# A fused sparse attention and gated MLP on one Trainium2 core: first pair loaded whole, another mask chain, mask rows by GpSimd and in query halves, in-projection dealt through the batch change

## The chip, the cores and the metric

The kernel runs on one core of a Trainium2 chip. A core has TensorE (PE, the matmuls; its weight loads are shown as PEld), VectorE (DVE), ScalarE (ACT), GpSimd (POOL) and SyncE (SP, which here only issues DMAs). Each engine executes its own instructions in the order in which they were emitted and waits on semaphores for the others. The metric is the device time of one execution in microseconds. Lower is better.

## What is computed

Block-sparse attention over 4 batches x 8 heads of 768 positions with head dimension 64, then a gated MLP with a spatial product. `sampled_blocks` gives three more allowed key blocks for each of 24 query blocks.

```python
scores = scale * np.matmul(q, k.transpose(0, 1, 3, 2))
mask = np.abs(blk_i - blk_j) <= window            # blocks of 32, window 1
mask = mask | (blk_i == 0) | (blk_j == 0) | (blk_i == n_blocks - 1) | (blk_j == n_blocks - 1)
for qb in range(n_blocks):
    for kb in sampled_blocks[qb]:
        mask[qb * block:(qb + 1) * block, kb * block:(kb + 1) * block] = True
scores = np.where(mask, scores, -1000000000.0)
attn = softmax(scores)
x = (attn @ v), heads side by side                # 768 x 512 for each batch
h = np.maximum(x @ w_in, 0.0)                     # 768 x 1024
u, v = h[..., :512], h[..., 512:]
v_n = (v - mean(v)) / np.sqrt(var(v) + 1e-06)
v_s = np.einsum('ts,bsd->btd', w_spatial, v_n) + b_spatial[None, :, None]
out = (u * v_s) @ w_out
```

## The kernel before

**Layout.** `qt_all` and `kt_all` hold, for each of 8 heads, the transposed queries and keys: rows 0 to 63 are the head dimension, rows 64 to 87 carry the mask. The mask is computed inside the score matmul: the 24 rows of k are the indicator of the key's block (`ind`), the 24 rows of q are the product of `bm` (24x24, 0 where allowed and -300 where not) with the indicator (the matmuls into `mq`). One score matmul has therefore 88 rows. The rows are the same for all heads, so head 0 gets them from ACT and the other heads are copied from head 0: heads 1 to 3 of k and 1 to 5 of q by DVE (`mask_rows`, L574), the others by DMAs on SP's queue (`mask_dma`, L579).

**The start.** Head 0 and head 1 of k and q are loaded one by one: the two of head 0 on ACT's queue, the others on SP's, behind the sampled blocks. `cast_qk` makes bf16 of them (q's head 0 on DVE, k's on ACT, head 1 of both on POOL), `tr_head` transposes on PE into a PSUM bank and copies to `kt_all` or `qt_all` on DVE. `keep_warm` issues matmuls whose result is not used. The mask chain on DVE runs from `ind` through `edge`, `diff` and `allowed` (three steps, one for each sampled block) to `bm` (L238).

**The first batch** is worked through in two query halves of 384 columns: 48 steps `g` of `qk_exp_half` (two score matmuls into one PSUM tile of two, L348, and one exponential on ACT, L352), with `av_half` six steps later (L364), the normalisation by the softmax sum on DVE (`rc` L375, `xn` L376) and at given steps the transposes of the next pairs (`tr_slots`, copies on DVE at L278) and of the results (`xtr_half`, L385 and the copy L386). From step 29 each step also issues one unit of the first MLP.

**The other three batches** are worked through by pairs of heads, 12 steps a pair: `qk_exp` (L313, exponential L317), `av` seven steps later (L329), `norm` (L394, L395). Pairs are loaded, cast by POOL (`prepare`, L124 and L127), transposed by DMA on SP's queue (`tr_dma`) and split into `kt_all` and `qt_all` by DVE (`split_pair`, L302, at s = 7 and 9 of the pair before). Step 48 (`N0`) is the first of the second batch.

**The MLP** of a batch is a list of units, `moe_q`, each one matmul of 512 columns (L472): 12 in-projection products of 4 units (v for the second half of the columns, u for the first), 6 spatial products of 6, 6 out-projection products of 4. They take turns over two PSUM banks. A v product is evicted to `vsb` by DVE (L485), followed by `stats` (L488) and `mv` (L489); after three v products POOL makes `rstd` (L492, L494) and three normalisations (`vn`, L499) are put into `norm_q` with the product count from which they may be emitted; they are emitted one at a time, in the middle of a product or after a u product. A u product is evicted by ACT (L509), the first of batch 0 by DVE (L506). The order of the products is a string for each batch. How many units a step gets follows from `slots_left`, which spreads the units left evenly:

```python
            if g == N0 + 7:
                slots_left = 50
            if moe_q and slots_left > 0:
                budget += len(moe_q) / slots_left
                slots_left -= 1
                while moe_q and budget >= 0.5:
                    moe_q.popleft()()
```

So no unit is issued in steps 48 to 54. The last batch's MLP follows after the last step, over more PSUM banks.

Of the kernel before, what the change touches and what calls it, by code (L numbers as in the profile page):

```python
# [10 lines left out]
FP32 = mybir.dt.float32  # L11
BF16 = mybir.dt.bfloat16
I32 = mybir.dt.int32
# [13 lines left out]
def kernel(  # L27
# [146 lines left out]
    nc.scalar.dma_start(out=stk[:, 0:1], in_=dram(k, 0, 0, 1))  # L174
    nc.scalar.dma_start(out=stq[:, 0:1], in_=dram(q, 0, 0, 1))
    nc.sync.dma_start(out=samp_i, in_=_listify(sampled_blocks).bitcast(I32))
    nc.sync.dma_start(out=stk[:, 1:2], in_=dram(k, 0, 1, 1))
    nc.sync.dma_start(out=stq[:, 1:2], in_=dram(q, 0, 1, 1))
# [6 lines left out]
    allowed = const.tile([NB, NB], FP32)  # L185
    tiny = const.tile([128, 1], FP32)
    nc.vector.memset(warm, 0.0)
    nc.gpsimd.memset(ind_nat, 0.0)
# [5 lines left out]
    def keep_warm(n, cols):  # L194
        for _ in range(n):
# [3 lines left out]
    keep_warm(8, 512)  # L199
# [4 lines left out]
    nc.gpsimd.affine_select(out=ind_nat, in_=ind_nat, compare_op=ALU.not_equal, fill=1.0,  # L204
                            base=0, pattern=[[-1, NB], [0, BLK]], channel_multiplier=1)
# [6 lines left out]
    colidx = const.tile([NB, NB], FP32)  # L212
    nc.gpsimd.iota(colidx, pattern=[[1, NB]], base=0, channel_multiplier=0,
                   allow_small_or_imprecise_dtypes=True)
    make_identity(nc, ident)
    for s in range(NG):
        nc.gpsimd.memset(vv[s][:, :, :, D:VA], 1.0)
    nc.gpsimd.memset(mhalf, -0.5)

    nat_tile(0, "q"), nat_tile(0, "k")  # L220
    nc.vector.tensor_copy(out=ind, in_=ind_nat.rearrange("b (p c) -> b c p", c=NCH))
# [3 lines left out]
    nc.vector.tensor_scalar(out=edge, in0=edge, scalar1=0.0, scalar2=None, op0=ALU.is_equal)  # L225
    nc.vector.tensor_tensor(out=diff, in0=diff, in1=diff, op=ALU.mult)
    nc.vector.tensor_scalar(out=allowed, in0=diff, scalar1=1.0, scalar2=edge,
                            op0=ALU.is_le, op1=ALU.max)
    nc.vector.memset(allowed[:, 0:1], 1.0)
    nc.vector.memset(allowed[:, NB - 1:NB], 1.0)  # L230
    samp_f = const.tile([NB, 2 * NR], FP32)
    nc.vector.tensor_copy(out=samp_f, in_=samp_i)
    for r in range(NR):
        nc.vector.scalar_tensor_tensor(out=allowed, in0=colidx,
                                       scalar=samp_f[:, 2 * r:2 * r + 1], in1=allowed,
                                       op0=ALU.is_equal, op1=ALU.max)
    bm = const.tile([NB, NB], BF16)
    nc.vector.tensor_scalar(out=bm, in0=allowed, scalar1=1.0, scalar2=-MASK_NEG,  # L238
                            op0=ALU.subtract, op1=ALU.mult)
    cast_qk(0, "q", slice(0, 1), nc.vector)  # L240
    cast_qk(0, "k", slice(0, 1), nc.scalar)
# [39 lines left out]
    tr_head(0, "k", dve_copy)  # L281
    act_copy(kt[0][D:KR, :], ind)
    mq = psum.tile([128, 1024], FP32, tag="sc", bufs=2, name="mq")
    for hf in range(2):
        nc.tensor.matmul(out=mq[0:NB, hf * 512:hf * 512 + HALF], lhsT=bm,
                         rhs=ind[:, hf * HALF:(hf + 1) * HALF], start=True, stop=True)
    act_copy(qt[0][D:KR, :].rearrange("p (b c) -> p b c", b=2),
             mq[0:NB].rearrange("p (b c) -> p b c", b=2)[:, :, 0:HALF])
# [150 lines left out]
    def moe_units(b):  # L439
# [19 lines left out]
        def normalize_next():  # L459
            if norm_q and norm_q[0][1] <= products[0]:  # L460
                normalize(norm_q.popleft()[0])

        def add(n, operands, post):
# [4 lines left out]
            def step(i):  # L468
# [5 lines left out]
                if i == n // 2:  # L474
                    normalize_next()
# [5 lines left out]
        def v_post(tcc, ps):  # L481
# [8 lines left out]
            if tcc % 3 == 2:  # L490
# [5 lines left out]
                norm_q.extend((i, products[0] + 2) for i in range(tcc - 2, tcc + 1))  # L496
# [7 lines left out]
        def u_post(tcc, ps):  # L504
            if b == 0 and tcc == 0:
# [4 lines left out]
            normalize_next()  # L510

        def in_proj(tcc, cols, post):
# [5 lines left out]
                 "v0 v1 u0 v2 u1 v3 u2 v4 v5 u3 u4 u5")  # L518
# [53 lines left out]
    def mask_rows(nm, h0, h1):  # L572
        t = kt_all if nm == "k" else qt_all
        nc.vector.tensor_copy(out=t[D:KR, h0:h1, :],  # L574
# [160 lines left out]
```

## Time and profile before

| | |
|---|---|
| median of 7 executions | 222.37 us (221.94 to 224.3) |
| the profiled execution | 222.73 us, its span 221.0 us |
| first scores start (L348) | 7.52 us |
| first scores of the second batch (L313) | 45.01 us |
| PE, ACT, DVE, POOL busy | 95%, 80%, 62%, 30% of the span |
| exponentials | 192: 48 at 813 ns (L352) and 144 at 814 ns (L317) |

How to read it: times in a timeline count from the start of the span. A line of it gives start, duration, engine, line of the kernel, operation, output and inputs by the program's names, shapes, count, and in brackets the idle time of the engine before it with what ended that. The durations of matmuls contain their pipeline, so the time from one start to the next says what a matmul costs PE. A line of the waits gives who waited for whom, microseconds in total, how often, and the longest.

### The profile page before, as it was taken

To read this page: it belongs to the slowest core of one execution; us is meant where nothing else is said; L and a number is where in the kernel's file an instruction comes from. 1 tells how busy PE (TensorE), PEld (TensorE's weight loads), DVE (VectorE), ACT (ScalarE), POOL (GpSimd) and SP (SyncE) were. 2 spreads that over 40 slices of the span, in tenths; PEclk is the share of its full clock that TensorE was granted. 3 is DMA by queue.
4 is the path that set the end of the run, shared out by engine and by line. 5 is a ranking of instruction groups with operands and counts; after the bars stand their busy time and mean duration, and the time that the engine had idled before them with its cause. 6 is when DMAs were issued, how large, how long until landed. Compare 5 with 4: busy or idle time off the path is not lost.

```text
span 221.0 us, 5258 instructions
## 1 busy us (share of the span) xinstructions
PE 209.6 (95%) x2088; PEld 126.9 (57%) x2122; DVE 138.0 (62%) x302; ACT 177.0 (80%) x245; POOL 66.5 (30%) x89
## 2 busy tenths in 40 slices
PE   7989999989999999999899999999899999999993
PEld 2667666655666666666555556665566665544551
DVE  5878438947985635377798535376896433675532
ACT  5689999989999889989879878888979885266351
POOL 6556879424086040400609001300602000022000
PEclk9999999999999999999999999999999999999999
DMA  6999999799994496979672466988321124620016
GB/s 183 338 297 396 393 291 332 164 147 359 274 271 94 140 245 190 286 231 296 203 199 89 82 123 221 223 279 219 68 42 32 30 50 85 227 86 0 0 55 230
DMA packets 59460, 41.26 MB, mean 187 GB/s; under 512 B 42524, under 2 KB 54956, under 8 KB 59436
## 3 DMA queue, kind: packets, MB, share of 16 engines
q1 hardware_dynamic: 59148, 40.54, 67.9%
q10 hardware_dynamic: 288, 0.39, 0.6%
q8 instruction: 16, 0.26, 0.5%
q14 instruction: 8, 0.07, 0.1%
HBM read 24.38 MB, written 6.29 MB: 139 GB/s over the span
## 4 chain that ended last, share of the span: by engine, by line
PE 78%; DVE 12%; ACT 4%; issue 2%; POOL 2%; POOLq 0%; ACTq 0%; DVEq 0%
PE ps_moe L472 30%; PE ps L313 19%; PE ps_av L329 12%; PE ps L348 5%; ACT a_all L317 4%; PE ps_sc L472 4%; PE ps_t L472 4%; DVE kt_all L302 3%; PE ps_av L364 2%; DVE kt_all L278 2%; DVE vsb L485 1%; DVE vn L499 1%; DVE qt_all L278 1%; ACT un L509 1%; DVE xn L376 1%
## 5 line engine op out<-in xcount | busy, mean ns | idle before, releaser
L317 ACT ACTIVATE a_all<-ps 128x768 bf16<-128x768 f32 x144 | 114.5, 814 | 16.6 <-PE ps L313 8.2
L313 PE MATMUL ps<-qt_all,kt_all 88*128 88x384 bf16 x288 | 70.4, 325 | 1.2 <-ACT a_all L317 0.8
L329 PEld LDWEIGHTS <-a_all 128*128 128x128 bf16 x864 | 46.1, 98 | 35.5 <-issue 2.2
L329 PE MATMUL ps_av<-vv,a_all 128*128 128x65 bf16 x864 | 50.9, 194 | 0.4
L472 PE MATMUL ps_moe<-w_in_t,xt 128*128 128x512 bf16 x144 | 45.0, 379 | 2.0 <-DVE vsb L485 1.3
L352 ACT ACTIVATE a_all<-ps 128x768 bf16<-128x768 f32 x48 | 35.5, 813 | 2.5 <-PE ps L348 2.1
L472 PE MATMUL ps_moe<-vn,w_spt 128*128 128x512 bf16 x110 | 33.6, 379 | 0.4
L472 PEld LDWEIGHTS <-xt 128*128 128x128 bf16 x192 | 18.6, 97 | 16.3 <-DVE xt L386 0.5
L492 POOL TENSOR_SCALAR std<-mv 128x3 f32<-128x3 f32 x8 | 1.9, 240 | 84.1 <-DVE mv L489 74.5
L535 DVE SCALAR_TENSOR_TENSOR gn<-ps_moe,b_col,un 128x512 bf16<-128x512 f32 x20 | 15.0, 750 | 17.1 <-PE ps_moe L472 12.6
L348 PE MATMUL ps<-qt_all,kt_all 88*128 88x384 bf16 x96 | 23.4, 325 | 1.5 <-DVE qt_all L278 0.8
L124 POOL CAST nat_k<-st_k 128x768 bf16<-128x768 f32 (+1 forms) x14 | 11.4, 818 | 40.5 <-DMA st_k<-in_k_dram 31.6
L472 PE MATMUL ps_moe<-w_out_t,gt 128*128 128x512 bf16 x73 | 21.3, 379 | 0.4 <-DVE gn L535 0.3
L313 PEld LDWEIGHTS <-kt_all 88*128 88x128 bf16 x288 | 19.2, 98 | 2.1 <-issue 1.1
L472 PEld LDWEIGHTS <-w_spt 128*128 128x128 bf16 x144 | 13.8, 97 | 10.5
L364 PEld LDWEIGHTS <-a_all 128*128 128x128 bf16 x288 | 15.1, 98 | 6.4 <-issue 0.3
L488 DVE BATCH_NORM_STATS2 stats<-vsb 128x6 f32<-128x512 bf16 x24 | 16.6, 693 | 1.5 <-ACT vsb L483 0.8
L364 PE MATMUL ps_av<-vv,a_all 128*128 128x65 bf16 x288 | 17.0, 194 | 0.2
L499 DVE TENSOR_SCALAR vn<-vsb,mv,rstd 128x512 bf16<-128x512 bf16 x24 | 13.4, 584 | 5.0 <-POOL rstd L494 4.8
L485 DVE TENSOR_SCALAR vsb<-ps_moe 128x512 bf16<-128x512 f32 x18 | 12.3, 684 | 4.6 <-PE ps_moe L472 4.6
L555 DVE COPY osb<-ps_moe 128x512 f32<-128x512 f32 x10 | 6.9, 692 | 11.5 <-PE ps_moe L472 8.0
L395 DVE TENSOR_TENSOR xn<-ps_av,rc 128x384 bf16<-128x384 f32 x24 | 13.4, 557 | 0.8
(98 smaller groups left out, 219.2 us busy)
## 6 DMA issues: line engine op xcount, KB each, us to landing
out_dram<-osb SPq DMA_DIRECT2D x24, 256.0 KB, 2.4
st_v<-in_v_dram SPq DMA_DIRECT2D x14, 384.0 KB, 5.4
st_k<-in_k_dram SPq DMA_DIRECT2D x13, 384.0 KB, 4.7
st_q<-in_q_dram SPq DMA_DIRECT2D x13, 384.0 KB, 4.0
wst<-in_moe_w_spatial_dram SPq DMA_DIRECT2D x3, 768.0 KB, 9.2
wst<-in_moe_w_in_dram SPq DMA_DIRECT2D x4, 512.0 KB, 9.6
wst<-in_moe_w_out_dram SPq DMA_DIRECT2D x2, 512.0 KB, 8.1
wst<-in_k_dram SPq DMA_DIRECT2D x2, 384.0 KB, 7.9
```

The costliest lines, as they stand in the source:

```text
L313: nc.tensor.matmul(out=ps[:, hf * 512:hf * 512 + HALF], lhsT=kt[j % H][:, ci * 128:(ci + 1) * 128], rhs=qt[j % H][:, hf * HALF:(hf + 1) * ...
L317: nc.scalar.activation(out=a_ref[j][:, ci, :].rearrange("p (b c) -> p b c", b=2), in_=ps.rearrange("p (b c) -> p b c", b=2)[:, :, 0:HALF], ...
L329: nc.tensor.matmul(out=av_ref[j][:, qc, :], lhsT=a_ref[j][:, ci, qc * 128:(qc + 1) * 128], rhs=vv[p % NG][:, h, ci, :], start=(ci == 0), s ...
L348: nc.tensor.matmul(out=ps[:, u * 512:u * 512 + HALF], lhsT=kt[j][:, ci * 128:(ci + 1) * 128], rhs=qt[j][:, grp * HALF:(grp + 1) * HALF], s ...
L352: nc.scalar.activation(out=a_ref["half", gh][:, 2 * i:2 * i + 2, :], in_=ps.rearrange("p (b c) -> p b c", b=2)[:, :, 0:HALF], func=AF.Exp, ...
L364: nc.tensor.matmul(out=av_ref["half", gh][:, qc, :], lhsT=a_ref["half", gh][:, ci, qc * 128:(qc + 1) * 128], rhs=vv[p][:, h, ci, :], start ...
L395: nc.vector.tensor_tensor(out=xn_ref[p][:, :, h, :], in0=ps[:, :, 0:D], in1=rc.to_broadcast([128, NCH, D]), op=ALU.mult)
L472: nc.tensor.matmul(out=box[0], lhsT=lhs, rhs=rhs, start=(i == 0), stop=(i == n - 1))
L485: nc.vector.tensor_scalar(out=vsb[:, tcc, :], in0=ps, scalar1=0.0, scalar2=None, op0=ALU.max)
L488: nc.vector.bn_stats(out=stats, in_=vsb[:, tcc, :])
L499: nc.vector.tensor_scalar(out=vn[:, tcc, :], in0=vsb[:, tcc, :], scalar1=mv[:, tcc, 0:1], scalar2=rstd[:, tcc:tcc + 1], op0=ALU.subtract, ...
L535: nc.vector.scalar_tensor_tensor(out=gn[:, tcc, :], in0=ps, scalar=b_col[:, tcc:tcc + 1], in1=un[:, tcc, :], op0=ALU.add, op1=ALU.mult)
```

## The change

- Pair 0 is loaded whole: k (both heads) on ACT's queue, q on SP's. k's head 0 is cast by DVE, k's copy after the transposes goes to ACT.
- The mask chain is split: a part without the sampled blocks (`static`) is made before `ind` is copied, then `hit` compares all three sampled blocks at once, `hits` reduces them, and `bm` follows. POOL makes its small index tiles before the indicator; the indicator's memset goes to DVE.
- The product with `bm` is made in two halves, each copied by ACT by itself, the second behind k's transposes. Six instead of eight warm-up matmuls of 512 columns, and three of 128 behind the first half.
- k's mask rows of heads 1 to 3 are copied by POOL from `ind`, those of 4 to 7 by a DMA from `ind`. q's rows are copied by DVE in query halves at steps 3, 6, 16 and 20 (`qt_mask`); q's DMA is gone.
- Pair 1's transposes of q all sit in step 3.
- Batch 0's units go on through steps 48 to 55, one a step, none in step 56; from step 57 the rest is spread over 48 steps. The first three u products of batch 0 are evicted by DVE.
- The time from which a normalisation may be emitted is counted in half products and lies half a product earlier, where a u product ends there; in batches 1 and 2 the product v5 comes after u3.

```diff
--- before.py
+++ after.py
@@ -171,21 +171,18 @@
     stage_two(("k", 2), ("q", 2))
     stage_two(("k", 3), ("q", 3))
     stage_two(("v", 2), ("v", 3))
-    nc.scalar.dma_start(out=stk[:, 0:1], in_=dram(k, 0, 0, 1))
-    nc.scalar.dma_start(out=stq[:, 0:1], in_=dram(q, 0, 0, 1))
+    nc.scalar.dma_start(out=stk, in_=dram(k, 0, 0, 2))
     nc.sync.dma_start(out=samp_i, in_=_listify(sampled_blocks).bitcast(I32))
-    nc.sync.dma_start(out=stk[:, 1:2], in_=dram(k, 0, 1, 1))
-    nc.sync.dma_start(out=stq[:, 1:2], in_=dram(q, 0, 1, 1))
+    nc.sync.dma_start(out=stq, in_=dram(q, 0, 0, 2))
     load(1, "kq")
     load(0, "v")
     load(2, "kq")
 
     ind_nat = const.tile([NB, S], BF16)
     ind = const.tile([NB, S], BF16)
-    allowed = const.tile([NB, NB], FP32)
     tiny = const.tile([128, 1], FP32)
     nc.vector.memset(warm, 0.0)
-    nc.gpsimd.memset(ind_nat, 0.0)
+    nc.vector.memset(ind_nat, 0.0)
     nc.vector.memset(tiny, 0.0)
     nc.scalar.activation(out=tiny, in_=tiny, func=AF.Exp)
 
@@ -196,49 +193,64 @@
             nc.tensor.matmul(out=wps[:, 0:cols], lhsT=warm[:, 0:128], rhs=warm[:, 0:cols],
                              start=True, stop=True)
 
-    keep_warm(8, 512)
-
-
-
-
-    nc.gpsimd.affine_select(out=ind_nat, in_=ind_nat, compare_op=ALU.not_equal, fill=1.0,
-                            base=0, pattern=[[-1, NB], [0, BLK]], channel_multiplier=1)
+    keep_warm(6, 512)
+
+
+
+
     diff = const.tile([NB, NB], FP32)
     nc.gpsimd.iota(diff, pattern=[[1, NB]], base=0, channel_multiplier=-1,
                    allow_small_or_imprecise_dtypes=True)
     row = const.tile([NB, 1], FP32)
     nc.gpsimd.iota(row, pattern=[[1, 1]], base=0, channel_multiplier=1,
                    allow_small_or_imprecise_dtypes=True)
-    colidx = const.tile([NB, NB], FP32)
-    nc.gpsimd.iota(colidx, pattern=[[1, NB]], base=0, channel_multiplier=0,
-                   allow_small_or_imprecise_dtypes=True)
+    colidx = const.tile([NB, 1, NB], I32)
+    nc.gpsimd.iota(colidx[:, 0], pattern=[[1, NB]], base=0, channel_multiplier=0)
+    nc.gpsimd.affine_select(out=ind_nat, in_=ind_nat, compare_op=ALU.not_equal, fill=1.0,
+                            base=0, pattern=[[-1, NB], [0, BLK]], channel_multiplier=1)
     make_identity(nc, ident)
-    for s in range(NG):
-        nc.gpsimd.memset(vv[s][:, :, :, D:VA], 1.0)
-    nc.gpsimd.memset(mhalf, -0.5)
-
-    nat_tile(0, "q"), nat_tile(0, "k")
-    nc.vector.tensor_copy(out=ind, in_=ind_nat.rearrange("b (p c) -> b c p", c=NCH))
+
     edge = const.tile([NB, 1], FP32)
     nc.vector.scalar_tensor_tensor(out=edge, in0=row, scalar=float(NB - 1), in1=row,
                                    op0=ALU.subtract, op1=ALU.mult)
     nc.vector.tensor_scalar(out=edge, in0=edge, scalar1=0.0, scalar2=None, op0=ALU.is_equal)
+    static = const.tile([NB, NB], FP32)
     nc.vector.tensor_tensor(out=diff, in0=diff, in1=diff, op=ALU.mult)
-    nc.vector.tensor_scalar(out=allowed, in0=diff, scalar1=1.0, scalar2=edge,
+    nc.vector.tensor_scalar(out=static, in0=diff, scalar1=1.0, scalar2=edge,
                             op0=ALU.is_le, op1=ALU.max)
-    nc.vector.memset(allowed[:, 0:1], 1.0)
-    nc.vector.memset(allowed[:, NB - 1:NB], 1.0)
-    samp_f = const.tile([NB, 2 * NR], FP32)
-    nc.vector.tensor_copy(out=samp_f, in_=samp_i)
-    for r in range(NR):
-        nc.vector.scalar_tensor_tensor(out=allowed, in0=colidx,
-                                       scalar=samp_f[:, 2 * r:2 * r + 1], in1=allowed,
-                                       op0=ALU.is_equal, op1=ALU.max)
+    nc.vector.tensor_scalar(out=static, in0=static, scalar1=1.0, scalar2=-MASK_NEG,
+                            op0=ALU.subtract, op1=ALU.mult)
+    for c in (0, NB - 1):
+        nc.vector.memset(static[:, c:c + 1], 0.0)
+    nat_tile(0, "q"), nat_tile(0, "k")
+    nc.vector.tensor_copy(out=ind, in_=ind_nat.rearrange("b (p c) -> b c p", c=NCH))
+    hit = const.tile([NB, NR, NB], FP32)
+    nc.vector.tensor_tensor(
+        out=hit, in0=colidx.to_broadcast([NB, NR, NB]),
+        in1=samp_i.rearrange("b (r t) -> b r t", t=2)[:, :, 0:1].to_broadcast([NB, NR, NB]),
+        op=ALU.is_equal)
+    hits = const.tile([NB, NB], FP32)
+    nc.vector.tensor_reduce(out=hits, in_=hit.rearrange("b r n -> b n r"), op=ALU.max,
+                            axis=mybir.AxisListType.X)
     bm = const.tile([NB, NB], BF16)
-    nc.vector.tensor_scalar(out=bm, in0=allowed, scalar1=1.0, scalar2=-MASK_NEG,
-                            op0=ALU.subtract, op1=ALU.mult)
-    cast_qk(0, "q", slice(0, 1), nc.vector)
-    cast_qk(0, "k", slice(0, 1), nc.scalar)
+    nc.vector.scalar_tensor_tensor(out=bm, in0=hits, scalar=0.0, in1=static,
+                                   op0=ALU.is_equal, op1=ALU.mult)
+    nc.scalar.activation(out=kt[0][D:KR, :], in_=ind, func=AF.Copy)
+    cast_qk(0, "k", slice(0, 1), nc.vector)
+
+    def kt_mask(h):
+        nc.gpsimd.tensor_copy(out=kt[h][D:KR, :], in_=ind)
+
+    def qt_mask(h0, h1, grp):
+        cols = slice(grp * HALF, (grp + 1) * HALF)
+        nc.vector.tensor_copy(out=qt_all[D:KR, h0:h1, cols],
+                              in_=qt_all[D:KR, 0:1, cols].to_broadcast([NB, h1 - h0, HALF]))
+
+    kt_mask(1)
+    cast_qk(0, "k", slice(1, 2), nc.gpsimd)
+    for s in range(NG):
+        nc.gpsimd.memset(vv[s][:, :, :, D:VA], 1.0)
+    nc.gpsimd.memset(mhalf, -0.5)
 
     def dve_copy(o, i):
         nc.vector.tensor_copy(out=o, in_=i)
@@ -278,14 +290,19 @@
                 nc.vector.tensor_copy(out=(qt if nm == "q" else kt)[(2 * p + h) % H][0:D, :],
                                       in_=ps[h * D:(h + 1) * D, :])
 
-    tr_head(0, "k", dve_copy)
-    act_copy(kt[0][D:KR, :], ind)
     mq = psum.tile([128, 1024], FP32, tag="sc", bufs=2, name="mq")
-    for hf in range(2):
+
+    def mask_product(hf):
         nc.tensor.matmul(out=mq[0:NB, hf * 512:hf * 512 + HALF], lhsT=bm,
                          rhs=ind[:, hf * HALF:(hf + 1) * HALF], start=True, stop=True)
-    act_copy(qt[0][D:KR, :].rearrange("p (b c) -> p b c", b=2),
-             mq[0:NB].rearrange("p (b c) -> p b c", b=2)[:, :, 0:HALF])
+        act_copy(qt[0][D:KR, hf * HALF:(hf + 1) * HALF],
+                 mq[0:NB, hf * 512:hf * 512 + HALF])
+
+    mask_product(0)
+    keep_warm(3, 128)
+    cast_qk(0, "q", slice(0, 1), nc.vector)
+    tr_head(0, "k", act_copy)
+    mask_product(1)
     tr_head(0, "q", dve_copy)
     keep_warm(6, 128)
 
@@ -456,8 +473,8 @@
         norm_q = deque()
         products = [0]
 
-        def normalize_next():
-            if norm_q and norm_q[0][1] <= products[0]:
+        def normalize_next(time):
+            if norm_q and norm_q[0][1] <= time:
                 normalize(norm_q.popleft()[0])
 
         def add(n, operands, post):
@@ -472,7 +489,7 @@
                 nc.tensor.matmul(out=box[0], lhsT=lhs, rhs=rhs,
                                  start=(i == 0), stop=(i == n - 1))
                 if i == n // 2:
-                    normalize_next()
+                    normalize_next(2 * products[0])
                 if i == n - 1:
                     post(box[0])
                     products[0] += 1
@@ -493,7 +510,7 @@
                                         scalar2=None, op0=ALU.add)
                 nc.gpsimd.tensor_tensor(out=rstd[:, cs], in0=std[:, cs],
                                         in1=mhalf[:, cs], op=ALU.pow)
-                norm_q.extend((i, products[0] + 2) for i in range(tcc - 2, tcc + 1))
+                norm_q.extend((i, 2 * products[0] + 3) for i in range(tcc - 2, tcc + 1))
 
         def normalize(tcc):
             nc.vector.tensor_scalar(out=vn[:, tcc, :], in0=vsb[:, tcc, :],
@@ -502,12 +519,12 @@
                                     op0=ALU.subtract, op1=ALU.mult)
 
         def u_post(tcc, ps):
-            if b == 0 and tcc == 0:
+            if b == 0 and tcc < NCH // 2:
                 nc.vector.tensor_scalar(out=un[:, tcc, :], in0=ps, scalar1=0.0,
                                         scalar2=None, op0=ALU.max)
             else:
                 nc.scalar.activation(out=un[:, tcc, :], in_=ps, func=AF.Relu)
-            normalize_next()
+            normalize_next(2 * products[0] + 1)
 
         def in_proj(tcc, cols, post):
             add(NDM, lambda g: (xt(g)[:, tcc * 128:(tcc + 1) * 128], w_in_t[:, g, cols]),
@@ -515,7 +532,7 @@
 
         order = ("v0 v1 u0 v2 u1 u2 v3 v4 v5 u3 u4 u5" if b == 0 else
                  "v0 v1 v2 v3 v4 v5 u0 u1 u2 u3 u4 u5" if last else
-                 "v0 v1 u0 v2 u1 v3 u2 v4 v5 u3 u4 u5")
+                 "v0 v1 u0 v2 u1 v3 u2 v4 u3 v5 u4 u5")
         for w, tcc in order.split():
             if w == "v":
                 in_proj(int(tcc), slice(DH, DFF), v_post)
@@ -569,26 +586,16 @@
     LAG0 = 6
     N0 = H * NCH
 
-    def mask_rows(nm, h0, h1):
-        t = kt_all if nm == "k" else qt_all
-        nc.vector.tensor_copy(out=t[D:KR, h0:h1, :],
-                              in_=t[D:KR, 0:1, :].to_broadcast([NB, h1 - h0, S]))
-
-    def mask_dma(nm, h0, h1):
-        t = kt_all if nm == "k" else qt_all
-        nc.sync.dma_start(out=t[D:KR, h0:h1, :],
-                          in_=t[D:KR, 0:1, :].to_broadcast([NB, h1 - h0, S]))
-
-    cast_qk(0, "k", slice(1, 2), nc.gpsimd)
     cast_qk(0, "q", slice(1, 2), nc.gpsimd)
+    kt_mask(2)
     prepare(1, "kq")
     cast_v(0)
-    mask_rows("k", 1, 2)
-    mask_rows("q", 1, 2)
-    mask_dma("k", 4, H)
+    kt_mask(3)
+    qt_mask(1, 2, 0)
+    nc.sync.dma_start(out=kt_all[D:KR, 4:H, :],
+                      in_=ind.rearrange("b (o n) -> b o n", o=1).to_broadcast([NB, H - 4, S]))
     load(1, "v")
     load(3, "kq")
-    mask_dma("q", 6, H)
     load(2, "v")
     load(3, "v")
     load_weights(NDM)
@@ -604,7 +611,7 @@
     load_weights(3)
 
     tr_slots = {}
-    for p, slots in ((1, (2, 2, 2, 3, 4, 4)), (2, (7, 7, 8, 9, 9, 10)),
+    for p, slots in ((1, (2, 2, 2, 3, 3, 3)), (2, (7, 7, 8, 9, 9, 10)),
                      (3, (13, 13, 14, 15, 15, 16))):
         for i, g in enumerate(slots):
             tr_slots.setdefault(g, []).append((p, "kq"[i // 3], i % 3))
@@ -626,11 +633,8 @@
             tr_head(1, "kq"[g], dve_copy)
         for p, nm, third in tr_slots.get(g, ()):
             tr_pair(p, nm, third)
-        if g == 1:
-            mask_rows("k", 2, 4)
-            mask_rows("q", 2, 4)
-        if g == 5:
-            mask_rows("q", 4, 6)
+        if g in (3, 6, 16, 20):
+            qt_mask(*{3: (2, 4, 0), 6: (4, 8, 0), 16: (1, 4, 1), 20: (4, 8, 1)}[g])
         if g == 28:
             tr_dma(4, "k")
             tr_dma(4, "q")
@@ -678,8 +682,10 @@
                 prepare(p + 2)
                 if p == 6:
                     cast_weights(2)
-            if g == N0 + 7:
-                slots_left = 50
+            if g < N0 + 9 and g != N0 + 8:
+                moe_q.popleft()()
+            if g == N0 + 9:
+                slots_left = 48
             if moe_q and slots_left > 0:
                 budget += len(moe_q) / slots_left
                 slots_left -= 1
```

## Prediction

> **What bounds the kernel now.** I read the page's busy shares first, then the chain that ended last, then what TensorE (PE) waits for once the first scores have started, and last the order of time around each of those waits.
>
> ```profile
> PE 209.6 (95%) x2088; PEld 126.9 (57%) x2122; DVE 138.0 (62%) x302; ACT 177.0 (80%) x245; POOL 66.5 (30%) x89
> PE 78%; DVE 12%; ACT 4%; issue 2%; POOL 2%; POOLq 0%; ACTq 0%; DVEq 0%
> ```
>
> PE is busy or on the chain nearly everywhere, and the change takes no product away. So time can only come from the start (before the first scores) and from the places where PE stands still. These are all of them from 6 us to the end:
>
> ```profile
> PE ps_moe L472 <- DVE vsb L485: 1.3, 2, 0.7
> PE ps L348 <- DVE qt_all L278: 0.8, 1, 0.8
> PE ps L313 <- ACT a_all L317: 0.8, 2, 0.6
> PE ps_moe L472 <- DVE gn L535: 0.3, 1, 0.3
> PE ps L348 <- DVE qt_all L244: 0.3, 1, 0.3
> PE ps L313 <- DVE qt_all L302: 0.3, 1, 0.3
> ```
>
> That is under 4 us, and idle time that a modelled matmul end covers comes on top (the start-to-start times below show it). The parts that the change touches, in order of time, are the start:
>
> ```profile
> 5.55 0.34 DVE L124 CAST nat_q<-st_q 128x384 bf16<-128x384 f32 x1
> 6.05 0.51 POOL L124 CAST nat_q<-st_q 128x384 bf16<-128x384 f32 x1 [1.19 <-DMA st_q<-in_q_dram]
> 6.83 0.55 DVE L244 COPY qt_all<-ps_moe 64x768 bf16<-64x768 bf16 x1 [0.47 <-PE ps_moe L262]
> 7.52 0.48 PE L348 MATMUL ps<-qt_all,kt_all 88*128 88x384 bf16 x2 [0.29 <-DVE qt_all L244]
> ```
>
> the change of batch:
>
> ```profile
> 45.01 0.50 PE L313 MATMUL ps<-qt_all,kt_all 88*128 88x384 bf16 x2 [0.28 <-DVE qt_all L302]
> 45.54 0.49 PE L313 MATMUL ps<-qt_all,kt_all 88*128 88x384 bf16 x2
> 46.78 0.48 PE L313 MATMUL ps<-qt_all,kt_all 88*128 88x384 bf16 x2 [0.56 <-ACT a_all L317]
> 47.48 0.48 PE L313 MATMUL ps<-qt_all,kt_all 88*128 88x384 bf16 x2
> ```
>
> and DVE's queue in the second batch's v products (in the third it is alike at 156 to 160 us):
>
> ```profile
> 106.59 0.90 DVE L499 TENSOR_SCALAR vn<-vsb,mv,rstd 128x512 bf16<-128x512 bf16 x1 [1.32 <-POOL rstd L494]
> 107.62 0.56 DVE L395 TENSOR_TENSOR xn<-ps_av,rc 128x384 bf16<-128x384 f32 x1
> 108.10 1.24 DVE L302 COPY kt_all<-tt_k 64x768 bf16<-64x768 bf16 x2
> 109.26 0.67 DVE L485 TENSOR_SCALAR vsb<-ps_moe 128x512 bf16<-128x512 f32 x1
> ```
>
> **PE's price list**, from start-to-start times where nothing waits: a score matmul 0.16, so 0.32 a step; six attention-times-values matmuls 0.195; a 512-column product (one unit) 0.216; a transpose 0.055. A step with no unit is 0.515 of PE, with one 0.73, with two 0.95. The exponential paces a step at 0.70. So in a step without a unit PE idles 0.19, and a unit put there costs 0.03 instead of 0.216.
>
> **The start: -0.2 us (-0.4 to +0.3).** Before, the first scores wait for the mask chain on DVE (bm at 5.46 to 5.63), then two mask products, q's transposes, DVE's copy. After, the mask chain begins before the indicator is there: some 2 us of small DVE operations (0.06 to 0.25 each by the rows of L223 to L238) from about 1.6, then ind (0.67), two new reductions (not in the trace; 0.2 each by the 24x24 rows, 0.52 at most by the longest of L234) and bm, by about 4.3 (5.0 at worst). What ends last is then q. Its whole pair is one 384 KB transfer on SP's queue; before, the same 768 KB of k and q had landed by 6.05 (POOL's row above; issued at 1.64, 4.4 us to landing), and k's and q's first heads by 3.1 and 4.45. I take k's pair at 4.3 and q's at 5.6 (4.9 to 6.05, the bytes are the same). From q: cast 0.34, transposes 0.5, copy 0.55, gaps 0.3, so scores at about 7.3 (7.1 to 7.8) against 7.52. k's copy on ACT (0.8 by the qt_all row of L247) ends near 6.7 and is hidden.
>
> **Mask rows in the first batch: about 0.** DVE loses the four copies of L574 ahead of pair 1 (0.97, 0.34, 0.63, 0.54) and gets a half-width one (0.2 to 0.3, or until POOL's cast ends, as the 0.97 row shows) and one of 0.34. The sixth step waited at 13.09 for DVE's q copy at 12.48 to 13.04; with less ahead of it that goes by 0.15 (0 to 0.3). POOL's three k copies (0.8 each, by the same bytes on ACT and POOL) fit into its waits for DMA before 11 us (1.2, 0.8, 0.2, 0.3); the dropped 72 KB mask transfer frees SP's queue for 0.83 and the transfers behind it by about 0.2. Against that, at step 16 a copy of 24x1152 (0.41, scaled from 0.54 for 1536) goes in front of head 3's reciprocal at 22.38, whose xn PE takes up at 23.01 with no slack: +0.45, and +1.1 if POOL's weight cast (1.04) is just running. The copy at step 20 (0.54) delays head 4's xn to about 25.4, not wanted before 26.3. Part of this is free: at 44.57 PE would have stood until 45.01 anyway, for DVE's chain behind POOL's casts to 41.03. Together the second batch starts at 44.8 instead of 45.01: the two parts together -0.2 (-0.6 to +0.5).
>
> **Units dealt through the batch change: -1.6 us (-1.0 to -1.75).** Before, steps 48 to 54 hold no unit and are paced by ACT. From the first scores of step 48 to those of step 57 (45.01 to 52.58) pass 7.57 us with four units; PE's prices give 9 x 0.515 + 6 transposes 0.33 + 4 x 0.216 = 5.83: 1.74 idle. After, eight of the steps carry one unit at 0.73 and outlast ACT's 0.70, so the idle time is filled. I take off 0.14 for steps where DVE is late: it also gets u1 and u2 (2 x 0.68) and the vn's (0.41 each) here, but it stood idle 1.4, 1.3 and 1.3 us between 46 and 52.6. Units left over are spread thinner, with no new wait.
>
> **Normalising half a product earlier: +1.1 us (+0.4 to +1.7).** In batches 1 and 2 the instruction order moves one more vn ahead of the pair split and the eviction of v3 (vsb). DVE waits for rstd there (1.32), so nothing starts earlier; the added vn comes after it. PE waits for just this eviction (0.7 each by the waits, 0.85 and 0.8 start to start). Batch 1: one vn of 0.41 alone, or 0.9 beside POOL's cast as in the row: +0.6. Batch 2: both vn's go in front (0.8 was behind the split already): 0.3 to 0.95, +0.5. Moving v5 behind u3 delays vn5 by a product, but it is due only five units into the spatial product: 0.
>
> **Sum.** Span 221.0 - 0.2 - 1.6 + 1.1 = 220.3; the profiled execution lies 1.73 above its span, so 222.03 against its 222.73. That execution is 0.36 above the median, so 221.7.
>
> [...] The eight warm-up matmuls start 0.43 apart and k's transposes after them 0.107; q's from 6.3 us run at 0.055, so PE reached full rate between 5.3 and 6.3. The change drops two of the eight and leaves gaps. By the rows alone PE is at full rate before the scores either way. [...]
>
> **The rivals.**
> A (the forecast, 0.44): as summed, 221.7.
> B (0.29): the evictions do not get later, because POOL's casts leave gaps in which vn and split run at 0.41 and 0.36 each. The row 108.10 speaks for it (one of the two copies was short), the 0.90 row against. 222.03 - 0.36 - 1.0 = 220.7.
> C (0.13), slower: PE stays at half rate through the first three steps. [...]
> D (0.14): the batch change is not filled, because DVE's u and vn hold up xn or the banks and PE waits there: 1.0 of the 1.6 is lost, 222.7.
>
> **The numbers.** About 0.5% (1.1 us) is what a measurement of this kernel can tell from no change; it puts the borders at 221.26 and 223.48. Faster: B nearly whole and a fifth of A, 0.34. Slower: half of C, a quarter of D and a little of A, 0.14. The rest is 0.52. The range 220.4 to 223.3 runs from B with a good start to D with a bad one and leaves out most of C.
>
> **What would show it.** Scores first at 7.1 to 7.8; bm before 4.5; steps 48 to 56 at 0.73 with no PE wait on ACT; one more vn between rstd and the vsb that PE waits for, and PE's waits on vsb at 2 to 2.7 us in total instead of 1.3. Wrong if the scores start below 7.0, if PE's waits on vsb do not grow, or if steps 48 to 55 still run at 0.70 with waits behind.

## The result and the profile after

The changed kernel is slower: median 225.86 us (222.84 to 228.46, 27 executions) against 222.62 us for the kernel before in the same sessions, a ratio of 1.0093 with a 95% interval of 1.0071 to 1.0115. (The ratio leaves out executions over 1.5% above the fastest of a kernel, so it is smaller than that of the medians.) The prediction was 221.7 (220.4 to 223.3), with 0.14 for slower.

The first thing to see is that the profile that came with the result does not show this. It is of the fastest of the 27 executions: 222.84 us, span 221.1, against 222.73 and 221.0 before. Its busy shares and its chain:

```profile
PE 207.7 (94%) x2089; PEld 126.3 (57%) x2123; DVE 137.4 (62%) x304; ACT 176.3 (80%) x244; POOL 68.9 (31%) x91
PE 72%; DVE 15%; ACT 5%; issue 2%; POOL 2%; DMA 1%; SPq 1%; POOLq 0%
```

PE has fallen from 78 to 72% of the chain and DVE has risen from 12 to 15%. The four longest of PE's waits from 6 us to the end (who waited for whom, us in total, times, longest):

```profile
PE ps_moe L489 <- DVE vsb L502: 2.1, 2, 1.1
PE ps L365 <- DVE qt_all L246: 0.9, 1, 0.9
PE ps L330 <- DVE qt_all L319: 0.6, 1, 0.6
PE ps_moe L402 <- DVE xn L393: 0.5, 1, 0.5
```

The waits on ACT at the change of batch (0.8) no longer stand in the list, those on vsb have grown from 1.3 to 2.1, and the waits for qt_all L319 and xn L393 are new. The start, in the timeline:

```profile
4.25 0.56 DVE L236 SCALAR_TENSOR_TENSOR bm<-hits,static 24x24 bf16<-24x24 f32 x1
4.87 0.33 PE L296 MATMUL mq<-ind,bm 24*24 24x384 bf16 x1 [0.95 <-DVE bm L236]
5.40 0.52 PE L274 MATMUL ps_moe<-ident,nat_k 128*64 128x128 bf16 x6
5.96 0.80 ACT L259 ACTIVATE kt_all<-ps_moe 64x768 bf16<-64x768 bf16 x1 [0.25 <-PE ps_moe L274]
6.67 0.55 DVE L256 COPY qt_all<-ps_moe 64x768 bf16<-64x768 bf16 x1 [1.32 <-PE ps_moe L274]
6.78 0.48 ACT L259 ACTIVATE qt_all<-mq 24x384 bf16<-24x384 f32 x1
7.27 0.49 PE L365 MATMUL ps<-qt_all,kt_all 88*128 88x384 bf16 x2 [0.20 <-ACT qt_all L259]
```

The scores start at 7.27 as forecast, and k's six transposes take 0.52, so PE is already at full rate here. But behind the sixth warm-up, issued at 3.28 and some 0.43 long, PE has nothing to do until the mask product at 4.87. The change of batch (step 48 starts at 44.79):

```profile
44.79 0.50 PE L330 MATMUL ps<-qt_all,kt_all 88*128 88x384 bf16 x2
45.13 0.38 PE L489 MATMUL ps_moe<-w_in_t,xt 128*128 128x512 bf16 x1
45.54 0.49 PE L330 MATMUL ps<-qt_all,kt_all 88*128 88x384 bf16 x2
46.56 0.49 PE L330 MATMUL ps<-qt_all,kt_all 88*128 88x384 bf16 x2
47.30 0.33 PE L402 MATMUL ps_moe<-ident,xn 128*128 128x128 bf16 x3
47.47 0.49 PE L330 MATMUL ps<-qt_all,kt_all 88*128 88x384 bf16 x2
```

and DVE's queue in the second batch's v products:

```profile
105.74 1.73 DVE L516 TENSOR_SCALAR vn<-vsb,mv,rstd 128x512 bf16<-128x512 bf16 x2 [1.32 <-POOL rstd L511]
107.61 0.56 DVE L412 TENSOR_TENSOR xn<-ps_av,rc 128x384 bf16<-128x384 f32 x1
108.08 0.71 DVE L319 COPY kt_all<-tt_k 64x768 bf16<-64x768 bf16 x2
108.71 0.68 DVE L502 TENSOR_SCALAR vsb<-ps_moe 128x512 bf16<-128x512 f32 x1
```

Two vn, 1.73 together, now lie between rstd and the eviction, where one of 0.90 lay. Against before, the scores of this execution are 0.25 earlier at step 0, 0.33 later at step 20, 0.21 earlier at step 48, 0.85 earlier at step 104, 0.55 at step 120 and 0.05 at step 168, and the span ends 0.11 later: gains and losses cancel. What makes the usual execution 3 us longer can only show in other executions.

**Theories.** T1: PE comes to full rate later in most executions, because the warm-up is thinner (six matmuls, then a stop). T2: something independent of the clock varies from execution to execution, such as DVE and POOL getting in each other's way.

### The profile page after: what moved, and what is told of

Read it like the earlier page. It is cut to its first block, busy times and chain, and to the rows that moved or that the text cites. A ratio compares the mean times of both kernels' runs of the same rounds, so it can differ in the third digit from the quotient of the medians.

```text
span 221.1 us, 5255 instructions
## 1 busy us (share of the span) xinstructions
PE 207.7 (94%) x2089; PEld 126.3 (57%) x2123; DVE 137.4 (62%) x304; ACT 176.3 (80%) x244; POOL 68.9 (31%) x91
## 4 chain that ended last, share of the span: by engine, by line
PE 72%; DVE 15%; ACT 5%; issue 2%; POOL 2%; DMA 1%; SPq 1%; POOLq 0%
PE ps_moe L489 28%; PE ps L330 17%; PE ps_av L346 10%; PE ps L365 5%; ACT a_all L369 4%; PE ps_sc L489 4%; PE ps_t L489 4%; PE ps_av L381 3%; DVE vn L516 3%; DVE vsb L502 2%; DVE stats L505 2%; DVE kt_all L319 1%; DMA xt<-xn 1%; DVE qt_all L319 1%; POOL rstd L511 1%
## 5 line engine op out<-in xcount | busy, mean ns | idle before, releaser
L489 PE MATMUL ps_moe<-w_in_t,xt 128*128 128x512 bf16 x144 | 45.5, 379 | 2.9 <-DVE vsb L502 2.1
L124 POOL CAST nat_k<-st_k 128x768 bf16<-128x768 f32 (+1 forms) x14 | 11.9, 851 | 40.7 <-DMA st_k<-in_k_dram 34.8
```

The lines of the kernel that those rows point to most:

```text
L489: nc.tensor.matmul(out=box[0], lhsT=lhs, rhs=rhs, start=(i == 0), stop=(i == n - 1))
```

## Experiments on the clock

**The changed kernel again** (no edit):

> The changed kernel unaltered, for a second profile and more times beside the kernel before. Its first profile has a span of 221.1 us with PE at full rate from about 4.3 us, which is no more than before, yet its median was 3 us higher. T1 (in most executions PE is released later, because the warm-up is thinner): a profiled execution of 224 us or more shows the first scores some 0.5 to 0.7 us later and the first steps at PE's half rate, 0.76 us more each until the release, and from about 12 us on the same times between stages as in the first profile. T2 (something else varies, such as DVE, GpSimd or DMA getting in each other's way): PE is at full rate before 6.5 us in every profile, and the extra time lies somewhere behind the first steps. Median 225 to 226 by both; executions spread over 222.8 to 228.

Median 227.12 (224.94 to 228.02), and the profiled execution took 227.91 us, span 226.1. PE's rows of its start (in all PE rows: start, duration, 128x128 or 88x384 is the moving tile, then the count):

```profile
4.88 0.49 PE L296 MATMUL mq<-ind,bm 24*24 24x384 bf16 x1 [0.96 <-DVE bm L236]
5.73 0.85 PE L274 MATMUL ps_moe<-ident,nat_k 128*64 128x128 bf16 x6
6.93 0.85 PE L274 MATMUL ps_moe<-ident,nat_q 128*64 128x128 bf16 x6
8.42 0.80 PE L365 MATMUL ps<-qt_all,kt_all 88*128 88x384 bf16 x2
14.85 0.85 PE L365 MATMUL ps<-qt_all,kt_all 88*128 88x384 bf16 x2
15.70 0.50 PE L365 MATMUL ps<-qt_all,kt_all 88*128 88x384 bf16 x2
```

The stop ahead of the mask product is the same to 0.01, but now the transposes take 0.85 instead of 0.52 and the scores 0.80 to 0.85 instead of 0.49: half rate, until 15.70. The trace's clock records say full rate from 15.71 here and from 4.34 in the first profile. The exponential of step 6 is 4.16 later and stays so until step 68. That is T1, and it accounts for 4.16 of the 5.07 by which this execution ends later. (The granted clock of the profile's own table reads 1.00 over these stretches: before the first record it takes full rate, so the rate is read from the durations.)

The rest of the 5.07 is of the kind of T2: 0.68 was got back at step 72, where the first profile's new wait (0.6 for qt_all L319) is missing, and 1.55 came between steps 151 and 152:

```profile
148.56 0.60 PE L489 MATMUL ps_moe<-w_out_t,gt 128*128 128x512 bf16 x2 [1.39 <-DMA gt<-gn]
```

`gt` is the gated product, transposed by DMA for the out-projection. The last one of batch 1 took 4.10 us from issue to landing instead of 2.46.

**Eight warm-ups in the changed kernel**

```diff
-    keep_warm(6, 512)
+    keep_warm(8, 512)
```

> The changed kernel with eight warm-up matmuls of 512 columns, as before, instead of six. T1: PE is released at the first opportunity in most executions as before, the median falls by about 3 us to 222.5 (222 to 223.3), the spread to about 1.5 us; the two more matmuls may delay the mask product by up to 0.4 us, hidden behind q. T2: 225 to 226, no change.

Median 224.36 (222.77 to 227.29). The profiled execution (222.97) has full rate from 3.83. Better by 2.8 than the six executions of the changed kernel beside it, and by 1.4 than the median of all 42 of its executions in the three sessions (225.72), but not the whole way: some executions still lie at 225 to 227. The stop until bm is still there (0.51); whether it is the reason was not tried by itself.

**Six warm-ups in the kernel before**

```diff
-    keep_warm(8, 512)
+    keep_warm(6, 512)
```

> The kernel before with six warm-up matmuls of 512 columns instead of eight, and nothing else. T1: the release comes later in many executions: median up by 1 to 3 us, to 223.5 to 225.5, and more spread. T2: no change, 222.4 to 222.8.

Median 224.11 (223.22 to 224.48), ratio 1.0050 (1.0023 to 1.0077); all twelve lie above the median of before, 222.77. Its profile has full rate from 10.60, the exponential of step 6 is 2.2 later than in the kernel before and the end 1.65. Two warm-ups that compute nothing are worth 1.3 us by the medians, 1.1 by the ratio. With them gone PE also stands for 0.93 ahead of the mask product, so their length and the stop change together here. The expected spread did not come: by the times nearly every execution is late, though only one was profiled.

**Ten warm-ups in one piece** (on the kernel with eight and the old normalisation, below)

```diff
-    keep_warm(8, 512)
+    keep_warm(10, 512)
...
     mask_product(0)
-    keep_warm(3, 128)
```

> As the run with eight warm-ups and the old normalisation, but ten warm-up matmuls of 512 columns in one piece up to the mask product, and the three of 128 columns behind it left out. PE is then at work without a gap from 1.2 to 5.4 us at half rate (4.6 with eight). T1: more executions are released early: lowest as before (221.6), median down from 223.0 to 222.2 (221.8 to 222.7). T2, or if eight were enough: no change, 223.0, or 0.2 more because the mask product comes later.

Median 222.07 (221.42 to 223.39) against 223.02 with eight: 0.95 less, as T1 says, with nothing above 223.4, where 6 of 12 lay with eight. The two runs are of different sessions, and their ratios to the kernel before, 0.9962 and 0.9984, have intervals that overlap; the three short warm-ups went too, so the step is not of the length alone.

**Twelve**

```diff
-    keep_warm(10, 512)
+    keep_warm(12, 512)
```

> [...] T1: no execution is released after 8 us, so the spread is under 1.5 us and the median 222.0 (221.6 to 222.5), although at half rate the mask product goes up to 0.9 later. If instead the length of the warm-up decides nothing beyond ten, its cost shows alone: 0.2 to 0.6 above the run with ten.

Median 222.73 (221.99 to 224.33), 0.7 above ten. In the profile the scores start 0.26 later than with ten and the difference is gone at step 6, so the span is the same; the spread is not smaller. That no execution would be released after 8 us was my estimate, and no run shows it. Beyond ten nothing is gained, which I had not expected.

**The changed kernel a third time** (no edit)

> The changed kernel unaltered, a third profile. T1: its span is 221.1 plus what the granted clock shows: 0.7 if PE is released at 6 to 8 us, 2 if at 9 to 11.5, 4.2 if at 12 to 16, plus 1.4 if the last gt of batch 1 lands late, plus up to 0.7 either way where DVE's copies meet GpSimd's casts. A time above that by over 0.7 would need another cause.

Median 225.18 (222.85 to 227.57). Profiled: 224.91, full rate from 11.86, the exponential of step 6 2.75 later than in the first profile, 0.69 got back at step 72, end 2.06 later. That leaves nothing to explain. My scale put 4.2 on a release at 12 to 16; at 11.86, just under it, 2.75 is between its steps. Over the three sessions 4 of 42 executions of the changed kernel were at or below 223.5: judged by the times, early release is its exception.

## Experiments on the other parts

**The normalisation as before**, on the changed kernel with eight warm-ups:

```diff
-                norm_q.extend((i, 2 * products[0] + 3) for i in range(tcc - 2, tcc + 1))
+                norm_q.extend((i, 2 * products[0] + 4) for i in range(tcc - 2, tcc + 1))
...
-            normalize_next(2 * products[0] + 1)
+            normalize_next(2 * products[0])
...
-                 "v0 v1 u0 v2 u1 v3 u2 v4 u3 v5 u4 u5")
+                 "v0 v1 u0 v2 u1 v3 u2 v4 v5 u3 u4 u5")
```

> The changed kernel with eight warm-ups and in addition the kernel before's time and order of the normalisations. By my sum the earlier normalisation costs 1.1 us, by the first profile after 0.8 (the two waits on vsb, 0.30 and 0.50): 0.8 to 1.1 below the run with eight warm-ups alone, about 221.6 if T1 holds, PE's waits on vsb back from 2.1 to 1.3 us in total. Rival B (the normalisations in front cost nothing): same as the run with eight warm-ups within 0.3.

Median 223.02 (221.64 to 225.12), 1.3 below the 224.36 with the new one; the lowest 1.1 below. (The 221.6 expected if T1 holds was not reached: half of the executions lie above 223.4.) PE's wait on vsb is back, here and in the run with eight warm-ups alone:

```profile
PE ps_moe L489 <- DVE vsb L502: 1.3, 2, 0.7
```

```profile
PE ps_moe L489 <- DVE vsb L502: 2.1, 2, 1.1
```

At step 120 it wins 0.30, at step 168 0.50. The profiled execution is one with full rate only from 10.28. It also shows what the copy of mask rows at step 16 can cost, DVE's row first and POOL's behind it:

```profile
24.17 1.31 DVE L246 COPY qt_all<-qt_all 24x1152 bf16<-24x1152 bf16 x1
25.72 0.36 DVE L393 TENSOR_TENSOR xn<-ps_av,rc 128x192 bf16<-128x192 f32 x1
```

```profile
24.03 1.04 POOL L167 CAST w_in_t<-wst 128x1024 bf16<-128x1024 f32 x1 [0.27 <-DMA wst<-in_moe_w_in_dram]
```

The cast began 0.14 before the copy and ended at 25.07; the copy ended 0.41 later, which is the price that I had put on it alone. (In the first profile, where it began as a cast ended, it took 0.55.) So it seems to have stood until the cast's end, and PE waited 1.3 for xn. Two copies of step 20 that began beside a cast did alike: they ended 0.40 behind its end in the first profile (1.05 long) and 0.41 in the run with ten warm-ups (1.25 long).

**The same with ten warm-ups**: the changed kernel's normalisation kept.

> The changed kernel, its earlier normalisation and its order of v5 and u3 kept, with ten warm-ups in one piece. Beside the run with ten warm-ups and the old normalisation (222.1) it differs in the normalisation alone, with most executions released early in both. By my sum 1.1 above it, 223.2, by the profiles of the pair with eight warm-ups 1.1 too, with PE's waits on vsb at 2.1 instead of 1.3. A second effect is possible: in batch 1 the last transposed gt lands 0.4 to 0.5 us before PE needs it with the new order and 1.1 to 1.8 with the old, and in one execution it landed late and PE waited 1.4: then some executions lie 1 to 1.5 higher still, median up to 223.8. If the normalisation costs nothing (rival B): 222.1.

Median 223.56 (222.96 to 224.50) against 222.07: 1.5 more. In the profile 0.29 of it lies at step 120 and 0.49 at step 168, on vsb as before. The slack of the last gt of batch 1 is 0.04 us here (0.39 to 0.53 in the other three profiles with the new order where it landed in time; 1.0 to 1.8 with the old). So 0.8 is shown in the waits. For the rest of the 1.5 there are two candidates, late gt's, seen in one profile, and a loss of full rate, which cost this profile 1.4 (last section); it stays open.

**The two late copies of mask rows moved**, on the run with ten warm-ups:

```diff
-        if g in (3, 6, 16, 20):
-            qt_mask(*{3: (2, 4, 0), 6: (4, 8, 0), 16: (1, 4, 1), 20: (4, 8, 1)}[g])
+        if g in (3, 6, 18, 21):
+            qt_mask(*{3: (2, 4, 0), 6: (4, 8, 0), 18: (1, 4, 1), 21: (4, 8, 1)}[g])
```

> The run with ten warm-ups, and in addition the two late copies of q's mask rows two steps and one step later (18 instead of 16, 21 instead of 20), behind the normalisation of heads 3 and 4. My sum had +0.45 (and +1.1 with a weight cast of GpSimd just running) at step 20, given back in part at step 48. If that is right: PE's wait for xn at 23 us (0.5 to 1.3) is gone, step 20 is 0.5 to 1.3 earlier, step 48 0.2 to 0.8, and the end too: median 0.2 to 0.8 below the run with ten warm-ups. Rival: the wait at step 48 takes all of it, no change at the end.

PE's wait for xn is gone, step 20 is 0.49 nearer to step 16, and the gain holds to the end: nothing is given back at step 48. Lowest 220.73 against 221.42. The median, 222.33 (220.73 to 224.13), does not show it: 4 of 12 lie above 223.4.

**Eleven warm-ups on that:**

```diff
-    keep_warm(10, 512)
+    keep_warm(11, 512)
```

> The run with ten warm-ups, old normalisation and moved mask rows, with eleven warm-ups. Its fastest execution was 220.7, its median 222.3 because 4 of 12 lay above 223.4. T1: one warm-up more lets fewer executions miss the release: lowest 220.8, median 221.5 (221.0 to 222.2). If the share of late ones does not depend on the eleventh: median 222.3 again.

Median 222.26, 221.44 to 223.55. The 221.5 that T1 had let me expect did not come; by the median the eleventh did not matter.

**The dealing undone**, on the run with ten warm-ups:

```diff
-            if g < N0 + 9 and g != N0 + 8:
-                moe_q.popleft()()
-            if g == N0 + 9:
-                slots_left = 48
+            if g == N0 + 7:
+                slots_left = 50
```

> The run with ten warm-ups, with the dealing through the batch change undone: no unit in steps 48 to 54, the rest spread over 50 steps from step 55, as in the kernel before. My sum gave the dealing 1.6 (1.0 to 1.75); the first profile after gave 0.55 by step 60 and 1.1 in all. So 1.0 to 1.2 above the run with ten warm-ups by the profile, 1.6 by the sum, 0.6 by rival D. Waits of PE on a_all at steps 50 to 56 back at 0.6 to 0.8.

Median 223.60 (222.40 to 225.67), 1.5 more; the lowest 1.0 more. In the profile the exponentials go from 2.53 behind at step 44 to 3.62 at step 104: 1.09. The first 2.53 have nothing to do with the edit, but show something else. PE waited 1.3 for xn at step 20, and then (stretch, its length, busy us of PE, PEld, DVE, ACT and POOL with counts, granted clock, DMA share, GB/s):

```profile
23.80:27.20 3.40, 1.96 (x28) 1.39 (x27) 2.88 (x5) 2.28 (x4) 2.80 (x3) 1.00 1.06 410
27.20:30.60 3.40, 3.40 (x27) 2.11 (x27) 1.39 (x5) 2.92 (x4) 2.37 (x3) 0.51 1.50 368
```

Half rate again for 3.41 us (0.51 in the second row), behind a stretch in which PE had been busy 1.96 of 3.40.

**The dealing alone**, in the kernel before:

```diff
-            if b == 0 and tcc == 0:
+            if b == 0 and tcc < NCH // 2:
...
-            if g == N0 + 7:
-                slots_left = 50
+            if g < N0 + 9 and g != N0 + 8:
+                moe_q.popleft()()
+            if g == N0 + 9:
+                slots_left = 48
```

> The kernel before with only the dealing through the batch change (with the first three u products of batch 0 on DVE): start, mask rows and normalisation as before, eight warm-ups. By the profile of the run without the dealing it is worth 1.1: median 221.5, lowest 220.9. By my sum 1.6: 221.0 and 220.4. Rival D (0.6): 222.0. The spread as in the kernel before, about a third of the executions 1.5 to 2 us higher.

Median 221.88 (220.81 to 223.47), ratio 0.9956 (0.9921 to 0.9992). The exponentials are 0.11 earlier than before at step 48 and 1.11 from step 104 on: 1.0 from the dealing, as by the ratio (0.44% of 222.45); by the medians it is 0.6.

**Nine and ten warm-ups on that:**

```diff
-    keep_warm(8, 512)
+    keep_warm(9, 512)       # 10 in the second
```

> The kernel before with the dealing, and nine instead of eight warm-ups. The mask product waits for bm until 5.68 anyway, and at half rate nine warm-ups and k's transposes end at 5.7. If the late executions of the run with eight (5 of 12 above 222.4) are late releases: fewer of them, median 221.4 (221.0 to 221.8), lowest 220.8 as before. If they have another cause: median 221.9, the same spread.

> As e13 with ten warm-ups, which at half rate delay the mask product by 0.4 and at full rate by nothing. Late releases as the cause: median 221.4 to 221.6, highest under 223. Another cause: 222.0 to 222.3, the spread as with eight.

Nine: median 221.45 (220.60 to 223.84), ratio 0.9943 (0.9911 to 0.9976). Ten: 221.54 (220.97 to 223.38), ratio 0.9933 (0.9903 to 0.9962). Both beat the kernel before and the changed one. By chance each profile is of its slowest execution, and both times the clock is the cause. Nine: half rate until 14.02, just as the transposes of the next pair's q begin:

```profile
12.52 0.85 PE L273 MATMUL ps_moe<-ident,nat_k 128*128 128x128 bf16 x6
13.16 0.85 PE L348 MATMUL ps<-qt_all,kt_all 88*128 88x384 bf16 x2
14.01 0.28 PE L273 MATMUL ps_moe<-ident,nat_q 128*128 128x128 bf16 x2
14.13 0.49 PE L348 MATMUL ps<-qt_all,kt_all 88*128 88x384 bf16 x2
```

Ten: full rate from 4.39, lost again after a wait of 1.8 for qt_all at step 6 (columns as above):

```profile
11.20:14.60 3.40, 1.65 (x19) 1.01 (x17) 3.24 (x6) 1.87 (x4) 1.38 (x3) 1.00 1.07 279
14.60:18.00 3.40, 3.40 (x35) 2.71 (x33) 1.75 (x5) 2.62 (x4) 2.58 (x3) 0.50 1.08 323
```

## Why the prediction was wrong, point by point

**The start: right in the one execution, wrong in the usual one.** bm is there at 4.81 (forecast before 4.5), the scores at 7.27 (7.3). The number hides two errors: bm came later than forecast, and what ended last was not q's copy (7.22) but ACT's of the second mask half (7.26), which stood behind k's. Where the clock comes late they start at 8.42.

**The clock: the step that failed.** The prediction said: "By the rows alone PE is at full rate before the scores either way." The rows did not carry that. The warm-ups' own spacing gave the end of six as 1.17 + 6 x 0.43 = 3.75, and my own sum gave bm as 4.3 or later: a stop of at least 0.55, measured 0.95. In three profiles of the changed kernel the release came at 4.34, 11.86 and 15.71. In the clock records, every stretch at full or half rate that lies whole in a trace here is a multiple of 3.413 us (215.04, 211.63, 20.48, 10.24, 3.41 among them); counted back from these three releases in whole multiples of it, the first point in the kernel is at 0.9, 1.6 and 2.1 us, different in each execution. So the rows of one execution could not show what the next would do.

**Rival C was what happened.** I gave it 0.13. By q's transposes (still 0.107 apart, 0.85 for the six) PE is at half rate there in two of three profiles. No run shows C's three steps: half rate covers two steps in one execution and five in the other, at 0.72 to 0.76 a step, and what PE does before the scores too (the scores start 1.15 later). It costs 2.75 and 4.16 us at step 6; of that, the stop at the sixth step hid nothing in the first and 0.24 in the second. On the kernel before, two warm-ups fewer cost 1.3.

**The mask rows: right in sum.** +0.45 at step 16, measured 0.5, and 1.3 beside a cast (forecast 1.1); step 48 at 44.79 (44.8).

**The dealing: right in kind, too large.** 1.6 was forecast, 1.0 and 1.09 were measured. Steps 48 to 56 of the kernel before with the dealing take 7.02 instead of 7.57 and hold eight units instead of four. (PE's weight loads show all eight; the record of one matmul, in step 51, is missing.) By the price list PE's work in them is 9 x 0.515 + 0.33 + 8 x 0.216 = 6.69: 0.33 idle remains where I took off 0.14. Nearly all of it lies in step 49, which takes 1.02 where I had 0.73 (step 50 takes 0.90, but three transposes of 0.055 are in it). And it is not DVE: in the first profile the scores of step 50 start at 46.56, 0.05 behind the end of ACT's exponential of step 48, which began only at 45.70. So a wait on ACT is left, under the modelled end of a matmul, where the list of waits does not show it. The larger part of the miss lies, in this pair, behind these steps: four units fewer there should have saved 4 x 0.216 = 0.86, but from step 57 to 104 this pair of profiles gains only 0.45. (In the pair with ten warm-ups, 0.33 is gained up to step 57 and 0.77 behind it.) Why is open.

**The normalisation: right.** +1.1 forecast; 0.8 in the waits, 1.1 to 1.5 by the times of the two pairs, PE's waits on vsb at 2.1 (2 to 2.7). Rival B falls with it; rival D had the direction of what the dealing fell short by, but not the cause: no wait on DVE stands there.

**The new wait at step 72** (0.6 for qt_all L319) was not forecast; it is in one of the three profiles of the changed kernel.

Put together from the first profile: 0.21 won up to step 48, 0.64 from there to step 104 (the dealing less the new wait), 0.80 lost on vsb, 0.16 lost behind: span +0.11, time +0.11 (222.84 against 222.73). Of the other 3 us of the median the two later profiles show the clock as the main part (2.75 and 4.16 at step 6), and one of them the late gt; that this holds for the executions without a profile is judged from their times.

## What to carry to other kernels

Look at the stops behind a warm-up as well as at its length: lay the times of the first real matmuls beside the end of the warm-up, and price a missed release at the half-rate time of everything that PE does until the next one. What the stop does apart from the length was not shown here, and filling it is no guarantee: with nine warm-ups and no stop behind them one execution was still late (14.02). A profile is one execution; where the median lies 3 us above it, look at what differs between executions before looking at what differs between kernels. An edit early in a kernel should be tried apart from one in its middle: here 1.0 us won at the batch change was hidden under a loss at the start. The rest of the change at the start and in the mask rows is not shown to gain anything: with ten warm-ups each, the kernel before with the dealing has a ratio of 0.9933 (0.9903 to 0.9962), and the changed kernel with the old normalisation 0.9962 (0.9934 to 0.9991).

## What the runs showed of the hardware

- **No share of busy time decides the first release in these profiles.** Counted back from the first release in stretches of 3.413 us, with PE's streaming time taken as columns at 0.83 ns (half rate, from the 0.427 us between the weight loads of the warm-ups of 512 columns; an estimate, since some matmul records are missing), stretches of 75 to 100% were followed by full rate (75% in the changed kernel's first profile, 79% with eight warm-ups), while others of up to 89% were followed by half rate (89% from 3.78 to 7.19 with nine warm-ups, 85% from 8.88 to 12.30 in the changed kernel). Those that failed above 79% hold few or no warm-ups of 512 columns, but transposes, mask products and scores. That these count less would not be all: the same six warm-ups, whole in one stretch and 75% of it, were followed by full rate in the changed kernel (0.93 to 4.34) and by half rate in the kernel before with six (0.36 to 3.78).
- **Full rate was lost in the middle of three executions without an idle stretch.** The three stretches of 3.41 us that led to half rate, all in the first batch, had PE streaming for 38, 43 and 45% of them, with a stop of 1.3 to 1.8 us in each; the next lowest of the first batch, 47, 49 and 52%, did not. In these three the stop cost itself and then 1.0 to 1.4 us more. Neither number is a threshold: a stop of 1.3 us in the run with ten warm-ups (47%) kept full rate, and so did stretches of 38 and 44% at the very end of two profiles (the dealing undone, 218.41 to 221.83; the changed kernel again, 220.51 to 223.92), where the last products run. In the changed kernel's start with ten warm-ups and the new normalisation it is seen so:

```profile
10.20:13.60 3.40, 1.88 (x20) 1.18 (x17) 3.23 (x6) 2.72 (x4) 2.72 (x5) 1.00 1.08 291
13.60:17.00 3.40, 3.38 (x34) 2.45 (x35) 1.26 (x3) 2.32 (x3) 3.06 (x4) 0.66 1.07 379
```

- **Three places at which executions were seen to part**: the release, this second loss, and a DMA that lands 1.6 us late behind a slack of 0.04 to 0.5. How much each has in the spread of the times was not counted.
